# Halving the first z block's chain over two engines, and triangular I = J pieces ahead of their columns' scores, in a gated attention and MLP kernel

## The chip, the cores and the metric

The kernel runs on one core of a Trainium2 chip. The metric is the device time of one execution in microseconds (us). All times "at 9.26 us" are counted from the start of the profiled span. The reported time of a run is 1.7 to 1.9 us longer than its span.

## The reference, cut to what matters

```python
batch, seq, d_model, d_qk = 8, 3008, 256, 64
scores = (1 / S) * z @ z.T              # per batch, S x S
attn   = np.maximum(scores, 0.0) ** 2
x      = u * (attn @ v)                 # 24064 x 256 over all batches
h      = x @ w_in                       # 256 -> 2048
out    = (h * np.cos(h)) @ w_out        # 2048 -> 256
```

The score matrix is symmetric: a piece of rows I and columns J, transposed, is the piece of rows J and columns I. This is what both kernels live on.

## The kernel before

A batch is six blocks of 512 tokens. Stage s works on one column of blocks J: TensorE multiplies the pieces of attn with v ("values", accumulated in banks `M` and one `E` buffer), while, between the products, it scores pieces that later stages need. A score goes from TensorE (`E`) to the scalar engine (ACT, relu, `r`) to the vector engine (DVE, square, `A`). POOL is the GpSimd engine; SP only issues DMAs here, among them all the DMA transposes. From stage 2 on, the MLP of earlier columns runs between the stages.

Pieces with I > J are transposed by DMA into their mirror image. A piece with I = J can be scored as a lower triangle of 128-blocks (`cut`); then three small DMA transposes fill in the upper blocks. For columns 0 to 2 of the first batch the kernel before scores everything that is not taken from a mirror in full.

```python
    groups = [
        (b, J, I, h)
        for b in range(B) for J in range(NC)
        for I in range(0 if b == 0 and J < 3 else J, NC)
        for h in range(2)
    ]
    ...
    def emit_score(later=None):
        b, J, I, h = groups[done_groups[0]]
        cut = I == J and not (b == 0 and J < 3)
        W = 2 * P if cut and h == 0 else width(J)
        ...                                      # two matmuls into E
        nc.scalar.activation(r[:, :, 0:W], e[:, :, 0:W], AF.Relu)
        ...                                      # DVE squares r into A
        if cut or (I > J and (b, J, I) not in direct):
            turns.append(((b, I), key))          # DMA transposes to be issued later
```

The start is written out by hand. Fillers are matmuls of zeros, meant to keep TensorE's clock up. `turn_on_pe(g)` transposes block g of z with TensorE into PSUM, `copy_turned(g)` copies it to SBUF:

```python
    turn_on_pe(0); copy_turned(0)                # ACT copies block 0, DVE the others
    turn_on_pe(1); copy_turned(1)
    emit_score(later=squares); emit_score(later=squares)
    turn_on_pe(2); copy_turned(2)                # in the bank of block 0, copied ahead of the squares
    squares.pop(0)(); squares.pop(0)()
    ...
    turn_on_pe(3); copy_turned(3)
    filler(2); emit_score(); filler(1); emit_score(); filler(1)
    ...
    phase_a_first(0, 12, {4: lambda: turn_late(4), 8: lambda: turn_late(5)})   # stage 0
    phase_a_first(1, 12)                                                       # stage 1
    nc.gpsimd.dma_start(w_out16, ...)            # 1 MB
    for i in range(2): emit_h(0, i)()            # first products with w_in
    phase_a_first(2, 14)                                                       # stage 2
```

## Time and profile before

| | before |
|---|---|
| time, median of the first three runs | 1192.81 us (1192.8 to 1194.91) |
| span of the profiled run | 1191.2 us |
| TensorE busy | 1183.7 us, 99 % |
| DVE, ACT, POOL busy | 85, 67, 57 % |
| granted TensorE clock, mean | 1.000 |

TensorE is the bound. Its line in the page's forty slices, and the clock that the throttle granted it, are full throughout (a digit is tenths of a slice of 30 us):

```profile
PE   9999999999999999999999999999999999999998
...
PEclk9999999999999999999999999999999999999999
```

### The profile page before, as it was taken

The page shows a single profiled execution, that of the slowest core. Times are in us where ns is not written, and L with a number is a line of the kernel's source. Part 1 is how long each engine was busy: PE and PEld are TensorE (multiplying, and loading weights), DVE is VectorE, ACT ScalarE, POOL GpSimd, SP SyncE. Part 2 cuts the span into 40 slices and gives each one's busy share as a digit, 9 for nine tenths or more (in the row PEclk, how much of TensorE's full clock was granted, in tenths as well). Part 3 has the DMA queues.
Part 4 walks back from the last instruction along what each step waited for, and adds up shares of the span by engine and source line. Part 5 has one row for each costly group of instructions (what it writes and reads, how often), then busy time and mean ns, then how long its engine had stood idle before and what let it go on. Part 6 is the DMA issues. An engine that isn't in the chain of part 4 may idle for free.

```text
span 1191.2 us, 29044 instructions
## 1 busy us (share of the span) xinstructions
PE 1183.7 (99%) x11887; PEld 726.8 (61%) x11887; DVE 1011.5 (85%) x1302; ACT 794.9 (67%) x927; POOL 679.0 (57%) x717
## 2 busy tenths in 40 slices
PE   9999999999999999999999999999999999999998
PEld 4556665665566656666566665656666566665566
DVE  6888888889988898888988889888888888888776
ACT  7966676667666676667676676666766666666454
POOL 3286745657466573755647556476555655545452
PEclk9999999999999999999999999999999999999999
DMA  9999999569995799955999469984798837974301
GB/s 160 175 172 158 115 171 130 102 122 104 173 127 101 123 137 166 126 89 103 155 152 130 86 106 158 168 123 70 120 162 152 122 72 120 173 122 84 65 20 54
DMA packets 449142, 148.00 MB, mean 124 GB/s; under 512 B 401264, under 2 KB 432496, under 8 KB 449008
## 3 DMA queue, kind: packets, MB, share of 16 engines
q1 hardware_dynamic: 368464, 112.93, 56.6%
q0 software_dynamic: 80032, 32.78, 27.7%
q8 instruction: 93, 1.52, 0.5%
q10 hardware_dynamic: 512, 0.43, 0.1%
q14 instruction: 41, 0.34, 0.1%
HBM read 66.32 MB, written 24.64 MB: 76 GB/s over the span
## 4 chain that ended last, share of the span: by engine, by line
PE 98%; ACT 1%; DVE 1%; issue 0%; POOL 0%; DVEq 0%; ACTq 0%
PE E L412 27%; PE M L490 23%; PE M L266 20%; PE E L266 19%; PE E L202 6%; PE M L533 1%; ACT r L212 1%; PE M L468 1%; DVE g L423 0%; PE E L673 0%; DVE sm L278 0%; PE E L533 0%; POOL s L441 0%; PE M L696 0%; ACT c L420 0%
## 5 line engine op out<-in xcount | busy, mean ns | idle before, releaser
L420 ACT ACTIVATE c<-E 128x1024 f16<-128x1024 f32 (+1 forms) x384 | 385.7, 1007 | 216.4 <-PE E L412 214.1
L423 DVE SCALAR_TENSOR_TENSOR g<-E,c 128x1024 f16<-128x1024 f32 (+1 forms) x384 | 458.9, 1197 | 62.0 <-ACT c L420 60.9
L212 ACT ACTIVATE r<-E 128x512 f16<-128x512 f32 (+1 forms) x342 | 328.0, 967 | 112.3 <-PE E L202 106.6
L266 PEld LDWEIGHTS <-v 64*128 64x128 f16 x4512 | 245.7, 94 | 229.6 <-issue 18.8
L412 PE MATMUL E<-x,w_in 128*128 128x512 f16 (+1 forms) x1408 | 354.0, 375 | 0.0
L441 POOL TENSOR_TENSOR s<-g 128x512 f16<-128x512 f16 (+1 forms) x184 | 207.8, 1130 | 189.3 <-DVE g L423 139.4
L266 PE MATMUL M<-A,v 64*128 64x512 f16 (+1 forms) x2256 | 283.0, 372 | 0.0
L266 PE MATMUL E<-A,v 64*128 64x512 f16 (+1 forms) x2256 | 278.0, 371 | 0.0
L442 POOL TENSOR_TENSOR g<-g 128x512 f16<-128x512 f16 (+1 forms) x184 | 219.0, 1190 | 14.4
L412 PEld LDWEIGHTS <-w_in 128*128 128x128 f16 x1536 | 133.1, 98 | 108.9 <-issue 19.5
L490 PEld LDWEIGHTS <-g 128*128 128x128 f16 x2816 | 172.5, 98 | 40.8
L217 DVE TENSOR_TENSOR A<-r 128x1024 f16<-128x1024 f16 x240 | 173.2, 734 | 15.1 <-ACT r L212 14.3
L294 POOL TENSOR_TENSOR x<-sm,uT 128x512 f16<-128x512 f32 (+1 forms) x43 | 48.6, 1131 | 223.5 <-DVE sm L278 223.5
L490 PEld LDWEIGHTS <-s 128*128 128x128 f16 x2112 | 129.4, 98 | 32.1 <-DVE s L448 0.5
L202 PE MATMUL E<-zT 64*128 64x512 f16 (+4 forms) x684 | 128.0, 356 | 1.6 <-DVE sm L278 0.7
L448 DVE TENSOR_TENSOR s<-s,g 128x1024 f16<-128x1024 f16 (+1 forms) x92 | 99.7, 1085 | 2.1 <-POOL s L441 2.1
L490 PE MATMUL M<-w_mix,s 128*128 128x128 f16 x1408 | 94.0, 219 | 0.3 <-POOL s L441 0.3
L490 PE MATMUL M<-w_mix,g 128*128 128x128 f16 x1408 | 93.6, 219 | 0.0
L490 PE MATMUL M<-w_out,g 128*128 128x128 f16 x1408 | 93.6, 219 | 0.0
L220 DVE TENSOR_TENSOR A<-r 128x512 f16<-128x512 f16 (+1 forms) x102 | 80.1, 785 | 8.6 <-ACT r L212 7.6
L202 PEld LDWEIGHTS <-zT 64*128 64x128 f16 x684 | 38.7, 94 | 38.4 <-issue 3.8
L450 DVE TENSOR_TENSOR s<-g,s 128x1024 f16<-128x1024 f16 (+1 forms) x92 | 60.6, 661 | 0.0
(58 smaller groups left out, 636.3 us busy)
## 6 DMA issues: line engine op xcount, KB each, us to landing
out_dram<-o SPq DMA_DIRECT2D x87, 256.0 KB, 2.1
v<-in_v_dram POOLq DMA_DIRECT2D x40, 256.0 KB, 11.5
u<-in_u_dram POOLq DMA_DIRECT2D x40, 256.0 KB, 4.5
A<-A SPq DMA_TRANSPOSE x252, 5.3
z<-in_z_dram POOLq DMA_DIRECT2D x14, 192.0 KB, 10.9
z<-in_z_dram POOLq DMA_DIRECT2D x14, 176.0 KB, 6.8
v<-in_v_dram POOLq DMA_DIRECT2D x8, 192.0 KB, 16.1
u<-in_u_dram POOLq DMA_DIRECT2D x8, 192.0 KB, 3.7
```

The source lines that it names most:

```text
L202: nc.tensor.matmul(e[:, t, 0:Wt], zT[rows, k * P:(k + 1) * P], zT[rows, J * CW:J * CW + Wt], start=True, stop=True,)
L212: nc.scalar.activation(r[:, :, 0:W], e[:, :, 0:W], AF.Relu)
L217: nc.vector.tensor_tensor(a4, r4, r4, ALU.mult)
L220: nc.vector.tensor_tensor(a4, r[:, :, 0:W], r[:, :, 0:W], ALU.mult)
L266: nc.tensor.matmul(bank[:, 0:width(J)], vs[b, k // 4][t * H:(t + 1) * H, k % 4, dh * P:(dh + 1) * P], value_rhs(b, J, k, t), start=start, ...
L412: nc.tensor.matmul(e[:, f, 0:W], w_in16[:, k, ft * P:(ft + 1) * P], x[:, k, 0:W], start=(k == 0), stop=(k == 1),)
L420: nc.scalar.activation(c[:, :, 0:W], e[:, :, 0:W], AF.Sin, bias=half_pi, scale=inv_s2)
L423: return lambda: nc.vector.scalar_tensor_tensor(gs[m][:, 2 * i:2 * i + 2, 0:W], e[:, :, 0:W], 1.0, c[:, :, 0:W], ALU.mult, ALU.mult)
L441: nc.gpsimd.tensor_tensor(s1[:, f, 0:n], g[:, f, low], g[:, lower, low], ALU.add)
L442: nc.gpsimd.tensor_tensor(g[:, f, low], g[:, f, up], g[:, f, low], ALU.subtract)
L448: nc.vector.tensor_tensor(s2[:, f, 0:n], s1[:, f, 0:n], g[:, f, up], ALU.subtract)
L490: nc.tensor.matmul(acc[:, k * P:(k + 1) * P], left[:, ft, k * P:(k + 1) * P], right[:, ft, :], start=(ft == 0 and k == 0), stop=(ft == F - ...
```

## The change

The intent has two parts. The first block's chain (cast, copy, relu) is to be shortened by giving half of each step to a second engine. And the I = J pieces of columns 1 and 2 are to be scored as triangles, which saves TensorE 0.11 us each. Their small transposes need time, so these pieces are scored first in their column.

```diff
-    turned = [... tag=f"M{i % 2}") for i in range(3)]
+    turned = [... tag=f"M{i}") for i in range(2)]
     turned_e = ppool.tile([P, 2, 2 * CW], FP16, name="turned_e", tag="E2")
...
+    def keys_of(b, J):
+        first = 0 if b == 0 and J < 3 else J
+        return sorted(range(first, NC), key=lambda I: (I != J, I))
...
-        cut = I == J and not (b == 0 and J < 3)
+        cut = I == J and (b > 0 or J > 0)
...
+        if shared:
+            nc.scalar.activation(r[:, 0, 0:W], e[:, 0, 0:W], AF.Relu)
+            nc.vector.tensor_scalar_max(r[:, 1, 0:W], e[:, 1, 0:W], 0.0)
...
                 emit_score(later=squares if s == 0 and i == lo else None)
+                if s < 2:
+                    emit_turns((0, s + 1))
...
         if g == 0:
-            nc.scalar.copy(dst, turned[g])
+            nc.vector.tensor_copy(dst[:, 0:T], turned[g][:, 0:T])
+            nc.scalar.copy(dst[:, T:CW], turned[g][:, T:CW])
...
-    cast_z(nc.vector, 0)
+    cast_z(nc.vector, 0, 0, 2)
+    cast_z(nc.gpsimd, 0, 2, 4)
...
+    emit_score(later=squares, shared=True)
     emit_score(later=squares)
-    emit_score(later=squares)
-    turn_on_pe(2)
-    copy_turned(2)
     squares.pop(0)()
     squares.pop(0)()
...
+    turn_on_pe(2)
+    copy_turned(2)
+    filler(1)
     turn_on_pe(3)
+    emit_score()
     copy_turned(3)
```

The copy of block 2 moves from ahead of two squares to behind them, and block 2 moves into the tile `turned_e` that block 3 also uses.

More of the change, by code (lines that the diff above doesn't have):

```diff
@@ L75 @@
     z32 = [z32_all[:, i, :, :] for i in range(NC)]
-    turned = [ppool.tile([P, CW], FP16, name=f"turned{i}", tag=f"M{i % 2}") for i in range(3)]
+    turned = [ppool.tile([P, CW], FP16, name=f"turned{i}", tag=f"M{i}") for i in range(2)]
     turned_e = ppool.tile([P, 2, 2 * CW], FP16, name="turned_e", tag="E2")
-    turned += [turned_e[:, 0, 0:CW], turned_e[:, 1, 0:CW], turned_e[:, 0, CW:2 * CW]]
+    turned += [
+        turned_e[:, 1, 0:CW], turned_e[:, 0, 0:CW],
+        turned_e[:, 1, CW:2 * CW], turned_e[:, 0, CW:2 * CW],
+    ]
     E = [ppool.tile([P, 2, CW], FP32, name=f"E{i}", tag=f"E{i}") for i in range(2)]
@@ L169, in turn_u @@
         uTs[s] = t
+    def keys_of(b, J):
+        first = 0 if b == 0 and J < 3 else J
+        return sorted(range(first, NC), key=lambda I: (I != J, I))
     groups = [
-        (b, J, I, h)
-        for b in range(B)
-        for J in range(NC)
-        for I in range(0 if b == 0 and J < 3 else J, NC)
-        for h in range(2)
+        (b, J, I, h) for b in range(B) for J in range(NC) for I in keys_of(b, J) for h in range(2)
     ]
@@ L188, with emit_score @@
     done_groups = [0]
-    def emit_score(later=None):
+    def emit_score(later=None, shared=False):
         b, J, I, h = groups[done_groups[0]]
         done_groups[0] += 1
-        cut = I == J and not (b == 0 and J < 3)
+        cut = I == J and (b > 0 or J > 0)
         W = 2 * P if cut and h == 0 else width(J)
@@ L211, in emit_score @@
         r = rpool.tile([P, 2, CW], FP16, name="r")
-        nc.scalar.activation(r[:, :, 0:W], e[:, :, 0:W], AF.Relu)
+        if shared:
+            nc.scalar.activation(r[:, 0, 0:W], e[:, 0, 0:W], AF.Relu)
+            nc.vector.tensor_scalar_max(r[:, 1, 0:W], e[:, 1, 0:W], 0.0)
+        else:
+            nc.scalar.activation(r[:, :, 0:W], e[:, :, 0:W], AF.Relu)
         def square():
@@ L650, with cast_z @@
     load_v(0, 0)
-    def cast_z(eng, g):
-        dst = z16s[0][:, 4 * g:4 * g + 4, :].rearrange("p k (t d) -> p k t d", t=2)
-        eng.tensor_copy(dst, z32[g].unsqueeze(2).to_broadcast([P, 4, 2, dqk]))
+    def cast_z(eng, g, lo=0, hi=4):
+        dst = z16s[0][:, 4 * g + lo:4 * g + hi, :].rearrange("p k (t d) -> p k t d", t=2)
+        eng.tensor_copy(dst, z32[g][:, lo:hi, :].unsqueeze(2).to_broadcast([P, hi - lo, 2, dqk]))
     def turn_on_pe(g):
@@ L659, in turn_on_pe @@
                 turned[g][:, k * P:(k + 1) * P], z16s[0][:, 4 * g + k, :], id16,
-                is_transpose=True, start=(k == 0 and g < 5), stop=(k == 3),
+                is_transpose=True, start=(k == 0 and g < 4), stop=(k == 3),
             )
@@ L673 @@
         nc.tensor.matmul(E[i % 2][:, 0, :], warm[:, 0:P], warm, start=True, stop=True)
-    cast_z(nc.vector, 0)
+    cast_z(nc.vector, 0, 0, 2)
+    cast_z(nc.gpsimd, 0, 2, 4)
     cast_z(nc.vector, 1)
+    turn_on_pe(0)
+    copy_turned(0)
     cast_z(nc.vector, 2)
@@ L681 @@
     squares = []
-    turn_on_pe(0)
-    copy_turned(0)
     turn_on_pe(1)
     copy_turned(1)
+    emit_score(later=squares, shared=True)
     emit_score(later=squares)
-    emit_score(later=squares)
-    turn_on_pe(2)
-    copy_turned(2)
     squares.pop(0)()
@@ L696, in filler @@
             nc.tensor.matmul(M[1], warm[:, 0:P], warm, start=True, stop=True)
+    turn_on_pe(2)
+    copy_turned(2)
+    filler(1)
     turn_on_pe(3)
+    emit_score()
     copy_turned(3)
     filler(2)
-    emit_score()
-    filler(1)
     emit_score()
```

## The prediction

> **What bounds the kernel now.** I read the page first, then a table of busy time by stretch, then the timeline of the first 50 us.
>
> The page's first part:
>
> ```profile
> PE 1183.7 (99%) x11887; PEld 726.8 (61%) x11887; DVE 1011.5 (85%) x1302; ACT 794.9 (67%) x927; POOL 679.0 (57%) x717
> ```
>
> TensorE (PE) is the bound: 1191.2 us of span less 1183.7 leaves 7.5 us idle. The table of stretches says where. Its columns: the stretch, its length, then the busy time of PE, weight loads, DVE, ACT, POOL, the granted clock, DMA.
>
> ```profile
> 5.00:10.00 5.00, 4.75 (x34) 1.66 (x32) 3.35 (x7) 4.18 (x5) 3.30 (x6) 1.00 0.84 106
> 10.00:20.00 10.00, 9.81 (x93) 4.87 (x92) 6.81 (x11) 8.45 (x9) 4.52 (x7) 1.00 1.15 162
> 20.00:25.00 5.00, 4.41 (x42) 2.14 (x39) 3.95 (x6) 4.99 (x7) 0.46 (x2) 1.00 1.08 180
> 35.00:42.00 7.00, 6.46 (x46) 2.57 (x44) 5.87 (x8) 6.03 (x8) 1.87 (x3) 1.00 1.09 173
> 42.00:60.00 18.00, 18.00 (x147) 10.99 (x142) 15.06 (x22) 16.69 (x20) 4.67 (x6) 1.00 1.27 183
> 200.00:1160.00 960.00, 960.00 (x9796) 593.73 (x9791) 824.19 (x1058) 632.76 (x738) 558.47 (x582) 1.00 0.83 120
> ```
>
> From 42 us to 1160 us PE never waits. The built program of the changed kernel has the same instructions in the same order there, up to names of buffers. So the change can only move the moment at which that rigid stream begins, and everything is decided before 48 us. The timeline of the start, which the first part of the change touches (start, duration, engine, line, what, count):
>
> ```profile
> 4.82 0.59 ACT L666 COPY zT<-turned 128x512 f16<-128x512 f16 x1 [1.06 <-PE turned L658]
> 5.46 1.03 PE L202 MATMUL E<-zT 64*128 64x512 f16 x4 [0.25 <-ACT zT L666]
> 6.11 3.77 ACT L212 ACTIVATE r<-E 128x1024 f16<-128x1024 f32 x4 [0.71 <-PE E L202]
> 6.43 0.40 PE L658 MATMUL turned<-id,z 128*128 128x128 f16 x4
> 6.66 0.39 PE L658 MATMUL turned_e<-id,z 128*128 128x128 f16 x4
> 6.86 0.42 DVE L668 COPY zT<-turned 128x512 f16<-128x512 f16 x1 [1.19 <-PE turned L658]
> 7.20 1.57 DVE L220 TENSOR_TENSOR A<-r 128x1024 f16<-128x1024 f16 x2
> 7.41 0.39 PE L202 MATMUL E<-zT 64*128 64x512 f16 x2
> 8.75 1.04 PE L266 MATMUL M<-A,v 64*128 64x512 f16 x8
> ```
>
> Block 2 of z is turned at 6.43, block 3 right behind it at 6.66, the third score group at 7.41, the value products at 8.75. The two other places where PE idles, in the same view:
>
> ```profile
> 25.07 0.39 PE L202 MATMUL E<-zT 64*128 64x512 f16 x2 [0.66 <-DVE sm L278]
> ...
> 39.88 0.39 PE L202 MATMUL E<-zT 64*128 64x512 f16 x2 [0.42 <-DVE g L423]
> ...
> 40.30 12.84 ACT L212 ACTIVATE r<-E 128x1024 f16<-128x1024 f32 x14 [0.82 <-PE E L202]
> ...
> 41.36 0.69 DVE L220 TENSOR_TENSOR A<-r 128x1024 f16<-128x1024 f16 x1 [0.41 <-ACT r L212]
> ```
>
> One score group takes from 39.88 to 41.36+0.69 = 42.05 us to become a squared piece: 2.17 us through PE, ACT and DVE.
>
> **What the Trainium skill says.** "PSUM — Partial Sum Buffer", section "PSUM bank collisions raise a hardware error": two engines must not touch one bank at once, even both reading, even in other columns. The 512 turned columns of a block are 1 KB, so they lie in one bank: halves of one copy on two engines cannot overlap. The kernel before never tries it, so no run here shows it yet; in the built program of the changed kernel the wait is there. "DMA: Bandwidth & Descriptors", section "Anatomy of one DMA — SWDGE (gpsimd) path": about 2 us of a DMA are fixed, mostly completion. The trace agrees for the small transposes of I = J pieces, at least 2.2 us to landing:
>
> ```profile
> L246 SPq DMA_TRANSPOSE A<-A x135: 1120/1185/2411, 62.5 to 1110.6; - x135
> ...
> DMA to landing us min/median/max: 2.2/3.9/9.3
> ```
>
> "TensorE: Matmul & The Clock Gate", section "What's actually happening": the clock rises after about 3.4 us of activity and falls after an idle window of that length. The trace agrees on the rise: matmuls of 512 columns start 0.427 us apart until about 6.4 us, 0.216 after. The gaps that I expect are under 2.3 us.
>
> **The change, part by part.** All times are in the trace's us; steps are end to start, some 0.04 us of semaphore included.
>
> 1. Cast in halves: gains nothing. The first transpose starts at 4.15, when the seventh filler ends (3.72 + 0.427), not when the cast ends (3.48 + 0.43 = 3.91).
>
> 2. Copy in halves: loses. ACT's half waits for DVE's half (bank). DVE half from 4.82, estimated 0.29 (0.42 for 512 columns, of which some 0.13 fixed), then ACT half, 0.59 less 0.21 = 0.38 (1024 elements take 1.02, so 256 cost 0.21): ends 5.53 instead of 5.41. First score 5.58 instead of 5.46, **+0.12**.
>
> 3. Relu in halves: in the built program DVE's half waits for ACT's half. ACT half 6.23 to 6.83, DVE half (0.68, as L278 of that size) to 7.55, first square from 7.58 instead of 7.20, second 0.60 later at 8.18.
>
> 4. The order of the copies: the costly step at the start. Block 2 is now turned into the tile that block 3 also uses. The fourth block's first transpose waits in the built program for DVE's tenth signal, which is the copy of block 2, and that copy now stands behind both squares: 8.18 + 0.60 = 8.78, + 0.42 = 9.20. So block 3 is turned at 9.24 instead of 6.66. From there PE's own work: score 9.56, two fillers, score 10.41, filler, value products 11.05 instead of 8.75. ACT: relu of the third group 10.0 to 11.02; DVE: its square 11.06, the copy of block 3 behind it 11.66 to 12.08; block 4 waits for that copy and is turned at 12.12 instead of 9.72. From there on as before: **+2.4 us** for the start, items 2 and 3 included.
>
> 5. Triangles: per column one score pair of 128 and 256 columns in place of 512: half of 0.216 = **-0.11 us** of PE, twice. ACT and DVE save 0.4 and 0.3 us each time, off the path.
>
> 6. Three small transposes per column. Column 1: its first product with the I = J piece follows four product pairs and a score into the column: 23.80 before, 23.80 + 2.3 = 26.1 after. The two squares it needs are those before at 20.22 and 21.18; after, they end near 22.6 and 24.15. SP issues take 1.19 each: 22.65, 24.18, 25.45. The loads of v and w_in, issued at 13.8 with 11.4 us to landing, are through at 25.2, so I take the least, 2.3 us, for the last: landed 27.75, wait 1.7 us. It contains the old wait of 0.82 us at 25.07 (DVE sm), so net **+0.86**. Column 2's transposes land near 46 to 49 us; item 7 delays their use beyond 50, so nothing.
>
> 7. Column 2's new order is I = 2, 0, 1, ...; the four groups that stage 1 scores ahead are then I = 2 and 0, while the products go I = 0, 1, 2. Piece I = 1 is scored inside stage 2, at 39.88 (first half), and used two product pairs later, where before only piece I = 2 came so late, used after sixteen. In the timescale of before: first half squared at 42.05; products 42.09 instead of 40.31; two pairs, then the second half's score 42.52 instead of 41.01; relu 42.95 to 43.97, square to 44.69, products 44.73 instead of 41.22: **+3.5 us**. The built program has these two DVE waits.
>
> Sum: 2.4 - 0.11 + 0.86 - 0.11 + 3.5 = +6.5 us. 1192.8 + 6.5 = 1199.3.
>
> **Rivals.** (a) The halves work as meant: the first relu ends 0.4 us sooner and the value products follow. For: ACT and DVE are idle before 6.11. Against: the waits in the built program, and at 8.43 PE ran fillers, so the relu was not what held 8.75. It would give about 1192. (b) Only the transposes hurt: landing at the maximum of 9.3 us instead of 2.3 makes item 6 cost up to 7 us more; for it speaks that DMA is busy (u landed 6 us after its transpose at 20.14), against it that the loads end by 25.2. Some 1202 to 1206. (c) The idle stretches cool the clock: for each 3.4 us at half rate 1.7 us more; the start, near the moment of the rise, is the likeliest. Some 1201. (d) Waits in series hide each other: if stage 1's and 2's overlap more than I count, 1196.
>
> **Range and chances.** The start's +2.4 and stage 2's +3.5 are chains of measured durations, each good to about 0.5 us. The transposes may cost 0 to 3, the clock 0 or 1.7. Runs of the kernel before spread by 2.1 us. I say 1199.5, range 1196.5 to 1203. Two per cent is 23.9 us, far above any of these: faster 0.005, same 0.98, slower 0.015.
>
> **What would show it.** The profile after should have: the ACT half of the copy starting after DVE's; a PE gap of about 2 us before the transposes of block 3, near 9.2; value products near 11; a PE wait for the DMA of an A piece near 26 to 28; two PE waits of 1.6 to 2.2 us for DVE squares early in stage 2, near 43 to 48; then no wait up to the last stage. If value products start before 9.5, item 4 is wrong; if PE does not wait for a square in stage 2, item 7 is. A PE wait at later stages for a piece's DMA would mean that SP's queue, longer by six issues of 1.2 us, was not free.

## The result, and the profile after

| | before | after |
|---|---|---|
| time, median of six runs each | 1193.18 us (1192.8 to 1197.65) | 1203.67 us (1203.42 to 1205.04) |
| ratio | | 1.0083, 95 % interval 1.0068 to 1.0099 |
| span of the profiled run | 1191.2 us | 1201.6 us |
| TensorE idle (span less busy) | 7.5 us | 13.5 us |
| granted clock, mean | 1.000 | 0.996 |

A ratio is the mean time of one kernel's fast runs over that of the other's fast runs of the same rounds, so it is not quite the ratio of the two medians.

The time lies 4.2 us above the predicted 1199.5 us and 0.7 us above the range's upper end. TensorE idles 6.0 us longer, but the span grew by 10.4 us, so some 4.4 us are not idle time. The same two rows of the page of the changed kernel show where to look:

```profile
PE   8899999999999999999999999999999999999998
...
PEclk9899999999999999999999999999999999999999
```

The second digit of the clock, 30 to 60 us, is an 8 where it was a 9. The record of the granted clock in the trace is finer. Before: 1.0 from 6.40 us to the end of the work, with no break. After: 1.0 from 6.72 us, **0.5 from 10.13 to 13.55**, 1.0 again, **0.5 from 47.68 to 54.51**, then 1.0 to the end of the work. Below, a stretch at 0.5 is called cold and one at 1.0 warm.

The timeline of the start of the changed kernel (start, duration, engine, line, what, and in brackets the idle time before it and who ended it):

```profile
4.82 0.29 DVE L675 COPY zT<-turned 128x256 f16<-128x256 f16 x1 [0.52 <-PE turned L667]
5.15 0.37 ACT L676 COPY zT<-turned 128x256 f16<-128x256 f16 x1 [1.38 <-DVE zT L675]
...
6.22 0.60 ACT L216 ACTIVATE r<-E 128x512 f16<-128x512 f32 x1 [0.70 <-PE E L205]
...
6.85 0.69 DVE L217 TENSOR_SCALAR r<-E 128x512 f16<-128x512 f32 x1 [1.07 <-ACT r L216]
7.57 1.29 DVE L227 TENSOR_TENSOR A<-r 128x1024 f16<-128x1024 f16 x2
...
8.78 0.42 DVE L678 COPY zT<-turned_e 128x512 f16<-128x512 f16 x1
9.26 0.38 PE L667 MATMUL turned_e<-id,z 128*128 128x128 f16 x4 [2.04 <-DVE zT L678]
...
11.74 1.89 PE L273 MATMUL M<-A,v 64*128 64x512 f16 x8
```

Read it downwards: the second half of the copy and of the relu each start when the first half is done. Two squares follow, then the copy of block 2, and only then may TensorE turn block 3, after 2.04 us of idling. Up to there the prediction is met to 0.05 us (9.24 predicted). The last line then is late: 11.74 instead of 11.05, and its eight products take 1.89 us where the same eight took 1.04 before. They run at half clock.

Stages 1 and 2, same view:

```profile
27.56 0.39 PE L273 MATMUL E<-A,v 64*128 64x512 f16 x2 [0.42 <-DVE A L227]
...
29.33 0.61 PE L273 MATMUL E<-A,v 64*128 64x512 f16 x4 [0.94 <-DMA A<-A]
...
46.64 0.61 PE L273 MATMUL M<-A,v 64*128 64x512 f16 x4 [1.62 <-DVE A L227]
...
49.31 1.04 PE L273 MATMUL M<-A,v 64*128 64x512 f16 x4 [1.85 <-DVE A L227]
```

The first two are in column 1: a wait for a square, which the prediction did not name, and the wait for column 1's transposes. The other two are for the squares of piece I = 1 of column 2. These last three were predicted. Four products take 0.61 us in the line at 46.64 and 1.04 us in the line at 49.31: the clock fell between them.

The table of stretches, cut here at the clock's own boundaries (columns: stretch, length, then busy time of PE, weight loads, DVE, ACT, POOL, the granted clock, DMA):

```profile
44.26:47.68 3.42, 1.43 (x10) 0.52 (x10) 1.92 (x3) 1.20 (x2) 0.54 (x1) 1.00 0.97 139
47.68:51.09 3.41, 1.78 (x10) 0.78 (x11) 0.69 (x1) 0.85 (x1) 0.00 (x0) 0.50 1.39 167
51.09:54.50 3.41, 3.41 (x20) 1.40 (x18) 1.19 (x2) 2.05 (x2) 0.00 (x0) 0.50 1.37 182
```

In the first stretch TensorE did 1.43 us of work out of 3.42, never idle for more than 1.62 us at once, and the next stretch ran at half clock. In the second it did 1.78 us of work at half clock, and the third ran at half clock too. The third was full, and the clock came back.

**Where the 10.4 us are.** I follow three marks through the traces: the turning of the fifth z block (9.72 before, 13.56 after, +3.84), the first product with w_in (36.40 and 40.93, +4.53), and the ninth product with w_in, which is the first after stage 2 (52.88 and 63.33, +10.45). Before, then after:

```profile
9.72 0.40 PE L658 MATMUL turned_e<-id,z 128*128 128x128 f16 x4
...
36.40 1.90 PE L412 MATMUL E<-x,w_in 128*128 128x512 f16 x8
...
52.88 1.90 PE L412 MATMUL E<-x,w_in 128*128 128x512 f16 x8
```

```profile
13.56 0.40 PE L667 MATMUL turned_e<-id,z 128*128 128x128 f16 x4
...
40.93 1.90 PE L421 MATMUL E<-x,w_in 128*128 128x512 f16 x8
...
63.33 1.90 PE L421 MATMUL E<-x,w_in 128*128 128x512 f16 x8
```

Behind the last nothing changes: the span is 10.4 longer. So the start lost 3.84, the way to the end of stage 1 another 0.69, stage 2 another 5.92. The prediction had 2.4, 0.75 and 3.4 for the three. What is over is 1.4 us at the start and 2.5 us in stage 2, at exactly the two places where the clock was at 0.5.

### The profile page after: what moved, and what is told of

It is laid out like the page before. It is cut to its first block, busy times and chain, and to the rows that moved or that the text cites. A ratio compares the mean times of both kernels' runs of the same rounds, so it can differ in the third digit from the quotient of the medians.

```text
span 1201.6 us, 29059 instructions
## 1 busy us (share of the span) xinstructions
PE 1188.1 (99%) x11887; PEld 729.6 (61%) x11887; DVE 1011.1 (84%) x1304; ACT 793.5 (66%) x927; POOL 678.8 (56%) x718
## 3 DMA queue, kind: packets, MB, share of 16 engines
q8 instruction: 93, 1.52, 0.5%
## 4 chain that ended last, share of the span: by engine, by line
PE 98%; DVE 1%; ACT 1%; issue 0%; DMA 0%; POOL 0%; SPq 0%; DVEq 0%; ACTq 0%
PE E L421 27%; PE M L499 23%; PE M L273 21%; PE E L273 19%; PE E L205 6%; PE M L542 1%; PE M L477 1%; ACT r L219 0%; DVE A L227 0%; PE E L683 0%; DVE g L432 0%; DMA A<-A 0%; PE E L542 0%; PE M L705 0%; POOL s L450 0%
## 5 line engine op out<-in xcount | busy, mean ns | idle before, releaser
L219 ACT ACTIVATE r<-E 128x1024 f16<-128x1024 f32 x341 | 326.5, 963 | 123.3 <-PE E L205 117.5
## 6 DMA issues: line engine op xcount, KB each, us to landing
z<-in_z_dram POOLq DMA_DIRECT2D x14, 192.0 KB, 10.4
```

## The experiments

My theory: the waits are those of the prediction, and two of them make TensorE's clock fall, though none lasts 3.4 us. The rivals: the clock falls for another reason and the waits have nothing to do with it; the halves themselves cost time; the excess comes from the transposes and their queue.

The stage 2 column below is the time from the first to the ninth product with w_in, 16.48 us in the kernel before. "Before" is the median of the kernel before, run again in the same session as the experiment.

| run | time, median | before | first w_in product at | stage 2 | clock |
|---|---|---|---|---|---|
| changed kernel | 1203.67 | 1193.18 | 40.93 | 22.40 | 0.996 |
| e1_start_only | 1197.15 | 1193.47 | 40.20 | 16.47 | 0.998 |
| e2_columns_only | 1200.22 | 1193.47 | 39.57 | 22.62 | 0.996 |
| e3_fill_start | 1202.08 | 1193.47 | 39.73 | 22.44 | 0.997 |
| e4_fill_both | 1202.90 | 1193.47 | 39.68 | 21.82 | 1.000 |
| e5_column1_only | 1198.39 | 1193.17 | 41.98 | 16.48 | 0.997 |
| e6_halves_only | 1193.34 | 1193.17 | 36.32 | 16.48 | 0.999 |
| e8_no_triangle2 | 1199.68 | 1193.17 | 40.06 | 20.03 | 1.000 |
| e9_w_out_later | 1217.95 (one look) | 1193.17 | 39.69 | 20.04 | 0.992 |
| e11_half_fill | 1199.47 | 1193.25 | 39.73 | 20.03 | 1.000 |
| e12_triangle2_old_order | 1206.05 | 1193.25 | 36.10 | 29.83 | 0.995 |

Marks, stages and clock are of each run's one profiled execution. The mean clock is rounded and takes in a cold end of the span after TensorE's last work (up to 1.9 us here), so a step of 0.001 in it can be that end alone.

### Each half of the change alone

The start alone: the columns' order and `cut` as before.

```diff
-        return sorted(range(first, NC), key=lambda I: (I != J, I))
+        return range(first, NC)
-        cut = I == J and (b > 0 or J > 0)
+        cut = I == J and not (b == 0 and J < 3)
-                if s < 2:
-                    emit_turns((0, s + 1))
```

> The changed start alone; both columns as in the kernel before. Theory (waits of the prediction's items 2 to 4, plus a cold clock that the wait at the start sets off): block 3 of z turned near 9.26 us after an idle of 2.0 us, 2.4 us of shift by the wait, then 3.41 us at granted clock 0.5 that adds 1.4 us: first values near 11.7, fifth block's turn near 13.6, the whole near 1192.9 + 3.8 = 1196.7 us. No idle over 0.5 us after 26 us and no second cold stretch. Rival (the clock is cold for a reason that has nothing to do with the wait, such as the doubled work of POOL and DVE at the start): the same here, but experiments that fill the wait would not warm it. Rival (the excess over the prediction comes from the columns alone): 1195.2 us here, no cold stretch.

Measured: 1197.15 us, 3.7 us over the kernel before. The clock is at 0.5 from 9.29 to 12.70 us and nowhere else while there is work, and stage 2 takes its old time. The start costs what the theory says, and on its own.

The columns alone: the start as in the kernel before (the diff's lines on `turned`, `copy_turned`, `cast_z`, `shared` and the order at the start undone).

> The start of the kernel before; triangles and the new order of columns 1 and 2 as in the changed kernel. Theory: a wait for the triangle's transposes near 26 us that nets +0.7 to +0.9 us, two waits for squares in stage 2 near 42 and 45 us that make +3.5 us, and a cold clock behind them that adds 1.7 to 2.5 us: 1198.9 to 1200 us, with one or two cold stretches of 3.41 us near 43 to 51 us, none at the start. Rival (the clock's fall belongs to the start only, and stage 2's excess comes from the DMA queue): waits for DMA in stage 2. If the clock stays warm here: 1197.2 us.

Measured: 1200.22 us, a little over the expected range. The two waits for squares are there, 1.62 and 1.85 us, with half clock behind them from 46.84 to 53.67 us. I missed one thing: with the start on time, column 1's transposes are waited for longer than in the changed kernel, and that wait cools the clock as well, from 26.36 to 29.78 us:

```profile
26.28 1.00 PE L270 MATMUL E<-A,v 64*128 64x512 f16 x4 [1.77 <-DMA A<-A]
```

This profiled run, 1201.92 us, is the slowest of its four; two others had a mean clock of 0.999 and were 1.5 to 1.8 us faster. But the fastest of the four, 1199.74 us, had 0.997, so losing less to the clock did not make these runs faster throughout; that the late transposes found in the run that fills both waits (below) take the clock's place would explain it, but these runs were not traced. By medians the two halves add up: 3.7 + 6.75 = 10.4 us, against 10.5 us for the whole change.

### Is it the halves or the order of the copies?

The three halvings kept; block 2 turned and copied where the kernel before does it, and both columns as before. Left out of the cut below: block 2 gets back a bank of its own, and block 3's copy, the third score and its fillers their old order.

```diff
     emit_score(later=squares, shared=True)
     emit_score(later=squares)
+    turn_on_pe(2)
+    copy_turned(2)
     squares.pop(0)()
     squares.pop(0)()
...
-    turn_on_pe(2)
-    copy_turned(2)
-    filler(1)
     turn_on_pe(3)
```

> Both columns as before, and the order of the blocks' turning and copying at the start as before (block 2 in the bank of its own, its copy ahead of the squares); only the three halvings (cast, copy, relu) are kept. Theory: the halves still follow one another (bank), cost 0.1 us at the first score and 0.4 us at the first square, no idle of 2 us before block 3, clock warm throughout: 1193.2 to 1194 us. Rival (the halves themselves cost the start's 2.4 us): 1195.5 us or more. Rival (halves gain as meant): 1192.7 us or less.

Measured: 1193.34 us, ratio 1.0002 (0.9987 to 1.0016). The halves neither cost nor gain. The first score starts at 5.57 us as in the changed kernel (5.46 before), but the value products start at 8.66 us (8.75 before). So the start's whole loss lies in the order of turning and copying and in the tile that blocks 2 and 3 share, not in the halves; the trace of the changed kernel puts it down to one copy, for which TensorE waits 2.04 us. Order and tile were not undone one without the other.

### Is it the wait that cools the clock?

Nine more fillers where TensorE waits at the start. They use up the wait; they do not remove it.

```diff
     copy_turned(2)
-    filler(1)
+    filler(10)
     turn_on_pe(3)
```

> The changed kernel with nine idle matmuls of 512 columns of zeros more on TensorE between the copy of block 2 and the turning of block 3, where it waits 2.04 us; the wait for the copy is kept. Theory (the idle cooled the clock): block 3 is still turned near 9.26 us, no cold stretch at 10 to 13.6 us, fifth block's turn at 12.1 us instead of 13.56, whole 1.4 us shorter than the changed kernel: 1202.2 us; stage 2's cold stretch stays. Rival (the cold stretch is not the idle's doing): no change, 1203.6 us.

Measured: 1202.08 us, as expected. Block 3 is still turned at 9.48 us, the clock stays at 1.0 from 5.68 to 46.64 us, and the first w_in product comes 1.20 us sooner. So the idle time was the cause of the cold stretch at the start.

The same, and in stage 2 fillers that add zeros into the open accumulators ahead of the two waiting products:

```diff
+            if s == 2 and i in (4, 6):
+                for _ in range(7 if i == 4 else 8):
+                    nc.tensor.matmul(M[i // 2 % 2], warm[:, 0:P], warm, start=False, stop=False)
```

> As the run before, and in stage 2 seven and eight idle matmuls of zeros, added into the open accumulators, ahead of the two products that wait 1.62 and 1.85 us for squares. Theory: both waits stay (the products start when the squares are done), but the clock never falls: TensorE is granted 1.0 from 6.7 us to the end, and what is left is the sum of the waits that the prediction counted, +6.5 us: 1199.3 us (1198.9 to 1200). Rival (part of the excess is no clock but longer waits): stays at 1201 us or more with the clock at 1.0.

Measured: 1202.90 us, **a miss**. In the profiled run (1201.59 us) the clock is at 1.0 from 5.62 us to the end, as meant. But stage 2 takes 21.82 us, not 20. A new wait has come up behind the two that were filled, for the three transposes of column 2's triangle (L253), which I had written off as hidden:

```profile
42.08 4.33 SPq L253 DMA_TRANSPOSE A<-A  x3
...
46.50 11.89 SPq L259 DMA_TRANSPOSE A<-A  x2
...
52.87 0.61 PE L273 MATMUL M<-A,v 64*128 64x512 f16 x4 [1.82 <-DMA A<-A]
```

In the changed kernel itself, the product that needs them starts at 54.66 us without a wait, because the half clock delays it anyway: the last of the three transposes lands about 1 us before it. Two costs lay side by side there, and taking one away shows the other. Two of the four runs of this kernel took 1203.95 and 1204.54 us at a mean clock of 0.998; they were not traced.

### What makes column 2's transposes late?

First without them: column 2's order kept, its I = J piece in full.

```diff
-        cut = I == J and (b > 0 or J > 0)
+        cut = I == J and (b > 0 or J > 2 or J == 1)
```

> Changed kernel with the idle matmuls at both places (as in the run that filled both), and column 2's order kept, but its I = J piece full instead of triangle, so that its three transposes are gone. Theory (with a warm clock, stage 2 next waits for these transposes): the wait of 1.82 us for a DMA near 52.9 us is gone, 0.1 us more of PE: the span 1.7 us shorter than that run's 1199.8, so 1199.9 us of time by the profiled run, clock 1.0. Rival (the wait is for other transposes): it stays near 1.8 us.

Measured: 1199.68 us, all four runs between 1199.21 and 1199.80. The wait is gone, the clock is at 1.0, and stage 2 takes 20.03 us: 3.55 us over the 16.48 of before. This kernel pays the waits that the prediction counted, with a warm clock, and it lands 0.2 us from the predicted 1199.5.

Then with the transposes, but with the load of w_out moved behind stage 2:

```diff
-    nc.gpsimd.dma_start(w_out16, ...)
     for i in range(2):
         emit_h(0, i)()
     phase_a_first(2, 14)
+    nc.gpsimd.dma_start(w_out16, ...)
```

> As the run that filled both, but the load of w_out (1 MB, issued at 42.4 us, in the same stretch as column 2's transposes) is issued after stage 2. Theory (the load takes the DMA engines from the transposes): the wait near 52.9 us falls from 1.82 us to under 0.5 us. Rival (the transposes are late by their own queue: the last of three is issued near 46.4 us and then takes its time): the wait stays over 1.3 us. In both a wait of some 9 us for w_out appears near 64 us, so the whole is longer and only the wait counts.

Measured: the wait of 1.82 us is gone, and stage 2 takes 20.04 us although all three transposes are there. They are issued at the same time, from 42.33 us (42.08 in the run that filled both), but land 2.5 to 4.4 us after their issue, where with the load beside them it was 7.4 to 7.8 us. So it is the 1 MB load that makes them late, as far as one execution of each kernel can show it. (The run as a whole is long, 1217.95 us, because w_out now comes late, as said beforehand.)

### Is column 2's order the cause in stage 2?

Column 2's order and form as before; the start and column 1's triangle stay.

```diff
-        return sorted(range(first, NC), key=lambda I: (I != J, I))
+        return sorted(range(first, NC), key=lambda I: (b == 0 and J == 2 or I != J, I))
-        cut = I == J and (b > 0 or J > 0)
+        cut = I == J and (b > 0 or J > 2 or J == 1)
```

> The changed kernel, with order and form of column 2 as before, so that the start and column 1's triangle are what is left of the change. Theory: no wait for squares and no cold stretch in stage 2; what is left is the start (2.4 and 1.2 to 1.4 us of clock) and column 1's transposes (+0.9): 1193.2 + 4.5 = 1197.7 us; first product with w_in near 40.9 us as in the changed kernel, ninth one (the first after stage 2) 16.5 us later, as before. Rival (stage 2 is late because stage 1 is late, whatever column 2's order): still 3 us or more are lost between those two, 1201 us or more.

Measured: 1198.39 us. Stage 2 is back at 16.48 us, to the hundredth. The rest is 0.7 us more than expected: in this profile the clock was at 0.5 for two stretches at the start, 7.85 to 14.67 us, where the changed kernel had one. How the same wait falls on the stretches differs between executions. The four runs spread from 1197.28 to 1201.53 us; only this one was traced.

### Does it take an idle stretch, or only a thin one?

In the kernel with column 2's full piece, about half of the fillers: 4 instead of 9 at the start, 3 and 4 instead of 7 and 8 in stage 2.

```diff
-    filler(10)
+    filler(5)
     turn_on_pe(3)
...
-                for _ in range(7 if i == 4 else 8):
+                for _ in range(3 if i == 4 else 4):
```

> As the run with full I = J piece of column 2, but with only about half of the idle matmuls: four instead of nine at the start, three and four instead of seven and eight in stage 2, so that TensorE still idles about 1.2 us near 9 us and about 1 us at each of the two waits for squares. Theory (the clock falls when the work streamed in a stretch of 3.41 us is below some share, which the traces so far put between 1.43 and 1.5 us of full-speed work): each stretch keeps over 1.9 us of work, so the clock is 1.0 throughout and the time the same as with the full filling, 1199.7 us. Rival (any idle of about 1 us may cool the clock): a cold stretch of 3.41 us, and 1.2 us or more of added time.

Measured: 1199.47 us with the clock at 1.0 throughout, although TensorE still idles:

```profile
9.21 0.38 PE L670 MATMUL turned_e<-id,z 128*128 128x128 f16 x4 [1.45 <-DVE zT L681]
...
11.03 1.04 PE L273 MATMUL M<-A,v 64*128 64x512 f16 x8
...
12.09 0.38 PE L670 MATMUL turned_e<-id,z 128*128 128x128 f16 x4
```

The value products start at 11.03 us and the fifth block is turned at 12.09 us; the prediction had 11.05 and 12.12. With a warm clock its start is right to 0.03 us. The two critical stretches of stage 2, in the table of stretches of this run:

```profile
43.50:46.92 3.42, 2.55 (x17) 0.83 (x13) 1.48 (x2) 1.63 (x2) 0.10 (x1) 1.00 0.86 156
46.92:50.33 3.41, 2.53 (x24) 1.28 (x24) 0.72 (x2) 1.49 (x3) 0.00 (x0) 1.00 1.42 219
```

Against the changed kernel's 1.43 us of work, 2.55 us keeps the clock up. Taking all profiled runs together, I worked out for each clock stretch of 3.41 us how long TensorE's records cover it, and counted that time by half where the clock was 0.5. Over thirteen profiles, all stretches at full clock with 1.43 us of work or less were followed by a cold one (among them those of 1.38 and 1.43 us in the changed kernel), and all with 1.88 us or more by a warm one. Between them are two: 1.59 us in e4_fill_both stayed warm, 1.62 us in e5_column1_only went cold, so my count is not exact to a few hundredths. Cold stretches were followed by a warm one from 1.52 us by this count, and stayed cold up to 1.18. So the limit here lies near 1.5 to 1.6 us of work in 3.41 us, 44 to 47 per cent. The length of the longest gap does not order the runs: e4_fill_both stayed warm over its gap of 1.82 us (the line at 52.87 above), and the changed kernel fell after one of 1.62 us. That the throttle counts in this way is a reading that fits these runs; no experiment isolates it.

### Could the triangle be had without the new order?

The start, and both columns' order, as before; only column 2's piece is a triangle, transposed as soon as it is scored.

```diff
-        cut = I == J and not (b == 0 and J < 3)
+        cut = I == J and (b > 0 or J > 1)
...
+                if s == 2:
+                    emit_turns((0, 2))
```

> The start and both columns' order as in the kernel before; only column 2's I = J piece is a triangle, transposed as soon as it is scored, which here is in stage 2. It asks whether the triangle could have been had without the new order. In the profile of before this piece is squared by 43.18 us and first used by the product at 44.02 us. Theory: three transposes behind the square, issued 1.2 to 1.5 us apart and landing 2.3 to 6 us after, make that product wait until 50 to 53 us: a PE wait of 5 to 9 us for a DMA, and one to three cold stretches behind it (1.7 us each, if so much work lies in them): 1200 to 1206 us. Rival (the transposes are hidden as all other pieces' are): no wait, 1193 us.

Measured: 1206.05 us, worse than the changed kernel. The wait is longer than I expected, because the queue that issues transposes is busy with five mirror pieces first:

```profile
30.91 18.57 SPq L256 DMA_TRANSPOSE A<-A  x5
49.59 3.77 SPq L250 DMA_TRANSPOSE A<-A  x3
...
55.68 1.04 PE L270 MATMUL M<-A,v 64*128 64x512 f16 x4 [11.78 <-DMA A<-A]
```

So neither of the two ways tried pays in column 2: the new order costs 3.55 us of waiting for 0.11 us of matmul, the old one a wait of 11.78 us.

### A version meant to beat both

The kernel before, with the first score of stages 1 and 2 three product pairs later, so that TensorE has work while DVE empties the buffer that the score needs.

```diff
-        lo, hi = 5 if s == 0 else 2, 42
+        lo, hi = 5, 42
```

> Not the change, but a version aimed at beating both kernels: the kernel before, with the first score of stages 1 and 2 put behind the sixth product pair instead of the third, so that TensorE has three product pairs to do while DVE empties the buffer that the score waits for. Theory: the waits of 0.66 us at 25.07 and of 0.42 us at 39.88 in the profile of the kernel before go to zero and nothing waits instead: 1.1 us less, 0.1 per cent, just at the edge of what the interval can show. Rival: the later scores make a later square be waited for (each is used some 16 pairs on), or the DVE's work of the other kind fills the place: no gain.

Measured: 1193.09 us against 1193.25 us, ratio 1.0008 (0.9988 to 1.0028): no gain shown. One of the six runs took 1201.42 us, for a reason that I did not trace. The wait of 0.66 us did go and that of 0.42 us fell to 0.26 us, but another came in its place five microseconds later, for a square that now stands behind other DVE work:

```profile
29.99 0.61 PE L266 MATMUL E<-A,v 64*128 64x512 f16 x4 [0.89 <-DVE A L217]
```

## Why the prediction was right or wrong

**Item 1 (cast in halves), right.** The first transposes start at 4.15 us before and after.

**Items 2 and 3 (copy and relu in halves), right in mechanism and times.** The halves follow one another (4.82 and 5.15 us, 6.22 and 6.85 us in the timeline above). The first score starts at 5.57 us instead of 5.46, the first square at 7.57 us (7.58 predicted). On their own they cost nothing (e6_halves_only, 1.0002), because the value products of the start come no later (8.66 us). In the changed kernel the later squares are part of item 4's wait.

**Item 4 (the order of the copies), right as a wait.** Block 3 is turned at 9.26 us (9.24). With the clock kept up, the fifth block is turned 12.09 - 9.72 = 2.37 us late (2.4 predicted). In the changed kernel it is 3.84 us late; the other 1.47 us are the cold stretch.

**Items 5 and 6, column 1, right in kind; the size came out right partly by luck.** The last transpose landed 2.4 us after its issue (2.3 assumed), and the net of triangle and wait is 0.69 us (0.86 - 0.11 = 0.75 predicted). But the working made one wait of 1.7 us, and the trace has 0.94 us for the DMA and 0.42 us for a square before it, 1.36 us together. And the old wait that it set against this is 0.66 us in its own line, not 0.82. The two errors nearly cancel. The size is not fixed either: with a warm clock (e11_half_fill) the same way costs 0.96 us, and with the start on time the DMA wait is 1.77 us (e2_columns_only). The section of the skill that the prediction sets beside the 2.2 us to landing is about DMAs issued from GpSimd; these transposes are issued from SP, so only the size agrees.

**Item 6, column 2 ("so nothing"), right only by accident.** The transposes land too late for a warm TensorE, by 1.82 us, because the load of w_out runs beside them (e9_w_out_later). It does not show in the changed kernel because the half clock is slower still. The estimate "land near 46 to 49 us" left the load out; they landed 7.1 to 7.4 us after issues between 43.5 and 46.5 us, the last by 53.9 us.

**Item 7 (column 2's order), right.** Its own cost is 20.03 - 16.48 = 3.55 us (3.5 predicted).

**The step that failed** is the sentence under the skill's heading: the clock "falls after an idle window of that length. ... The gaps that I expect are under 2.3 us." From this followed that the clock would stay up, and rival (c) was left as one possible stretch worth 1.7 us. In truth the gap of 2.04 us at the start (2.48 and 2.73 us in e1_start_only and e5_column1_only) and the one of 1.62 us in stage 2 were enough to bring the clock down, and the one of 1.85 us kept it down. This was so in all three profiles of kernels that kept the waits in stage 2 unfilled, and in all three that kept the one at the start. The clock, priced at 0 or 1.7 us, cost 1.47 us at the start and 22.40 - 20.03 = 2.37 us in stage 2. Of these 2.37 us the clock alone is not the whole: with it warm and the transposes still late, 1.8 us of them came back as a wait for a DMA. No run has the cold clock without column 2's transposes. The parts 2.37 + 1.47 + 0.69 + 3.55 + 2.37 make the 10.45 us of the last mark by construction, since each is a difference of marks; what stands against the prediction is 2.4, 0.75 and 3.4 us, 6.5 in all. Its sum gave 1199.3 us, and it said 1199.5 without a reason for the 0.2.

**The rivals.** (a), halves that work, is refuted. (b), late transposes, came true for column 2 and was hidden; column 1's landed as counted. (c) happened, at the place I named and at one that I did not. (d), waits that hide each other, did not lower the sum of waits, but it is the reason why warming the clock in stage 2 gave only 22.44 - 21.82 = 0.62 us as long as the transposes stood behind it.

**The range** would have held 1203.67 us if two cold places had been priced as likely rather than one as possible: 1199.5 + 1.5 + 2.4 = 1203.4.

What stays open: the runs of 1205.0 us of the changed kernel had a mean clock of 0.994 instead of 0.995 to 0.996. One more cold stretch, at 1.7 us, would fit, but no trace of such a run exists.

## What to carry to other kernels

When you price a wait of the engine that is the bound, price the clock behind it too: here 2.0 us of waiting cost 1.5 us more, and 3.5 us cost 2.4 us more, and a handful of matmuls of zeros in the waits saved both where no other wait stood behind (e11_half_fill, which has no triangle in column 2). Moving one copy behind two squares cost 2.4 us, and splitting three steps in two gained nothing that could be measured; look first at which copy frees the tile that the bound engine needs next. And when an experiment takes one cost away and the time hardly moves, look for the next wait in the trace before giving up the theory: here a late DMA lay exactly under the slow clock.

## What the Trainium skill lacked or had wrong

- "TensorE: Matmul & The Clock Gate", section "Why this matters for your kernels", advises against idle gaps of over about 3 us, and the table in "What's actually happening" has the clock fall after at least one idle window of about 3.4 us. Here the clock fell after stretches in which no gap was longer than 2.04 us (at 10.13 us) or 1.62 us (at 47.68 us). What fits is the share of work in a stretch of 3.41 us: 1.43 us and less was followed by half clock, 1.88 us and more was not, and of two stretches near 1.6 us one was. The page's section "A second HAM failure mode: psum-queue depth-cycling" does tell of a kernel whose clock oscillates because of short idles between groups of matmuls, but gives no length or share for them. A rule by share would have caught this.
- The same page, "What's actually happening", says that the window is free-running. The trace agrees: the changes at 10.13, 13.55, 47.68 and 54.51 us lie whole multiples of 3.41 us apart. The page draws from it that the number of slow matmuls at a kernel's start varies from run to run. What it doesn't say is that a wait inside a kernel varies likewise: the same wait can cost one stretch in one execution and two in another (e1_start_only and e5_column1_only have the same start; one had 3.41 us at half clock there, the other 6.83).
- "DMA: Bandwidth & Descriptors", section "Anatomy of one DMA — SWDGE (gpsimd) path", gives the fixed 2 us of a DMA issued from GpSimd. The pages also give a bandwidth for DMA transposes. I found on no page how long small transposes from SBUF to SBUF take beside a load or behind others of their own queue, and that decided two runs: the 1 MB load beside three small transposes made TensorE wait 1.82 us for them (no wait without the load), and five queued transposes held the issuing queue for 18.57 us.
